# Weights in larger pieces on one queue, and the last attention job of segment 0 with its output projection one step sooner

## The chip, the cores and the metric

The kernel runs on one core of a Trainium2 chip. The metric is the time of the device in microseconds, from the start to the end of one execution; a profiled execution also gives the span from the first to the last instruction, and a record of every instruction. The engines are TensorE (PE; its weight loads are listed apart as PEld), VectorE (DVE), ScalarE (ACT), GpSimd (POOL) and SyncE (SP), which here only issues DMAs and DMA transposes.

## The reference

One block of a transformer for 2048 tokens of width 448 in bf16. A conditioning vector gives scales and shifts for two layer norms and gates for two residuals. The attention has 16 heads of width 28 and works in 4 segments of 512 tokens: inside a segment it is causal, and across segments it reads a memory that is summed up from the keys and values of the segments before.

```python
mod = (_silu(c) @ w_mod).reshape(c.shape[0], 6, 1, -1)      # sa, ca, ga, sb, cb, gb
h = _layernorm(x) * (1 + ca) + sa
x = x + ga * _A_ref(h, A_wq, A_wk, A_wv, A_wo, A_beta)
h = _layernorm(x) * (1 + cb) + sb
x = x + gb * _B_ref(h, B_w_gate, B_w_up, B_w_down)

# in _A_ref, for each segment s, with phi(t) = t + 1 if t > 0 else exp(t)
p = softmax(qs @ ks^T * scale + mask);  a_dot = p @ vs
a_mem = (phi(qs) @ M) / (phi(qs) @ z + 1e-6)
o = g * a_mem + (1 - g) * a_dot
M = M + phi(ks)^T @ vs;  z = z + phi(ks).sum
# in _B_ref
h = sigmoid(x @ w_gate) * (x @ w_up);  out = h @ w_down
```

## The kernel before

**Tiles.** Activations lie as 128 tokens by 448 columns (x_sb, four tiles to a segment) or transposed, as hT with the 448 columns in four chunks (k) of partitions by 512 tokens. Heads go in four groups of four; a pair (s, hc) names head group hc of segment s. PSUM has four rotating banks for everything but the logits, all from the pool ps_m: a matmul group that takes a bank waits until its last user was evacuated, four groups earlier. The logits have a buffer of their own (lg) of four banks, one buffer: a group of logits waits for the exponential of the group before.

**Head of the program.** The weights Wq, Wk, Wv and the first modulation columns are loaded, the first layer norm is taken, and the weights are multiplied by the scale of the layer norm (pad_copy, line 657, by DVE for Wq and Wk: chunks 0 to 3 of Wq, then Wk) while PE makes the bias rows (bias_rows, line 664) from the unscaled weights. Wq and Wk are first staged in the buffer that later holds the Down weights, so in the profile they are named wd_sb. The DMAs of a program share eight completion semaphores in turn: one that is issued waits on the eighth before it.

**Loop.** For each segment s, each head group hc and each group g of key blocks (block 0; blocks 1 and 3; block 2): logits, then ACT takes the exponential into pT, then GpSimd sets the masked corner of each block to zero (mask, line 437). For a head group that is done with its logits there follow, during the next one: mem_read (phi of the queries times the memory, tile mem, evacuated by DVE as r, t at lines 478 to 482), pv (probabilities times values, 40 matmuls into acc, evacuated as r, t at lines 457 to 463), the sum of both into ou (464), and otr (the transpose of ou into oT, issued on SP, 498).

**Order.** The program is not scheduled by a tool: the Python order is the order on each engine. Between logits and the rest a queue of jobs, fill, is run: the projections of later segments, the memory update dM, Wo, Gate, Up and Down. run_fill takes jobs until their costs have used up the pace of the step. Work on DVE and GpSimd that nothing on PE needs at once is put off with later(ns, fn, tag), and done when a counted clock (tick) has passed its due time, or when need(tag) asks for it. The masks are due 2600 ns after their logits, phi 4300 after its exponential.

**Around the change.** The queue at segment 1 starts with the last V projection of segment 2, the q and k projections of segment 3 for group 0, the memory update and prep_b2 (the columns of LN2). At step (1, 0, 2) the planner rebuilds the queue: two of the jobs that are left, then the four Wo tiles of segment 0 (wo_jobs), then memory keys, the rest, and Gate and Up. wo_tile multiplies oT by Wo for 128 tokens into pwo, and wo_fin adds the residual (520), takes the statistics (269, 270), the inverse root on GpSimd (rs, 273 and 274), and puts off the normalization xn (277, 281), each followed by a transpose into hT on SP (287). After the last tile four modulations of hT on DVE (291) are put off by 6500 ns and more. The first Gate matmul (gps, 542) reads hT, and Up (ups, 547 and 559) follows.

```python
                if prev[0] >= 0 and (g == 1 or ...) and prev in todo:
                    todo.remove(prev)
                    pv(*prev)
```

Of the kernel before, what the change touches and what calls it, by code (L numbers as in the profile page):

```python
# [13 lines left out]
P = 128  # L14
# [3 lines left out]
def kernel(  # L18
# [16 lines left out]
    nc = tc.nc  # L35
    _, S, D = A_x.shape
# [7 lines left out]
    DP, LW = NK * P, D - 3 * P  # L44
# [22 lines left out]
    def m_f32(name):  # L67
        return ps_m.tile([P, 512], F32, tag="m", name=name)
# [7 lines left out]
    def later(ns, fn, tag):  # L76
        deferred.append((clock[0] + ns, len(deferred), fn, tag))

    def run_deferred(pick):
        while True:  # L80
            due = [d for d in deferred if pick(d)]
            if not due:
                return
            d = min(due, key=lambda d: d[:2])
            deferred.remove(d)
            d[2]()

    def tick(ns):
        clock[0] += ns
        run_deferred(lambda d: d[0] <= clock[0])  # L90

    def need(*tags):
        for tag in tags:
            late_ = [d for d in deferred if d[3] == tag]
            if late_:
                print("forced", tag, len(late_), max(d[0] for d in late_) - clock[0])
            run_deferred(lambda d: d[3] == tag)
# [39 lines left out]
    wq_st = wd_sb[:, 0:NK, :]  # L137
    wk_st = wd_sb[:, NK:2 * NK, :]

    def load_w(eng, dst, w):  # L140
        eng.dma_start(dst[:, 0:3, :], w[0:3 * P, :].rearrange("(k p) n -> p k n", p=P))
        eng.dma_start(dst[0:LW, 3, :], w[3 * P:D, :])
# [6 lines left out]
    for b in wm_bufs:  # L149
        nc.vector.memset(b[:, NK * D:], 0.0)  # L150
    for st, w in ((wq_st, A_wq), (wk_st, A_wk)):
        other = nc.scalar if w is A_wq else nc.sync
        nc.sync.dma_start(st[:, 0:2, :], w[0:2 * P, :].rearrange("(k p) n -> p k n", p=P))
        other.dma_start(st[:, 2, :], w[2 * P:3 * P, :])
        other.dma_start(st[0:LW, 3, :], w[3 * P:D, :])
    load_w(nc.sync, wv_sb, A_wv)

    def load_wo():
# [25 lines left out]
    for hs in range(4):  # L184
        nc.gpsimd.affine_select(out=bmask[:, :, hs, :], in_=bmask[:, :, hs, :], compare_op=ALU.is_ge,
                                fill=0.0, base=-HP * hs, pattern=[[0, NHC], [0, ME]], channel_multiplier=1)
        nc.gpsimd.affine_select(out=bmask[:, :, hs, :], in_=bmask[:, :, hs, :], compare_op=ALU.is_ge,
                                fill=0.0, base=HP * hs + Dh - 1, pattern=[[0, NHC], [0, ME]],
# [251 lines left out]
    def pv(s, hc):  # L440
        u = (s, hc)
        need(("mask", u))
        pT = pT_of.pop(u)
        vt = vt_all[s]
        acc = m_f32("acc")
        accv = acc[:].rearrange("p (t h e) -> p t h e", h=4, e=HP)
        for qb in range(TPS):
            for hs in range(4):
                for kb in range(qb + 1):
                    c0 = OFF[kb] + (qb - kb) * P  # L450
                    nc.tensor.matmul(accv[:, qb, hs, 0:ME], lhsT=pT[:, hs, c0:c0 + P],  # L451
                                     rhs=vt[:, kb, hc * 4 + hs, 0:ME], start=(kb == 0), stop=(kb == qb))
        ou = ou_bufs[(s * NHC + hc) % 2]
        ou_of[u] = ou
        ouv = ou[:].rearrange("p t h e -> p (t h) e")[:, :, 0:Dh]
        r1 = work.tile([P, TPS, 4], F32, tag="r1", bufs=2)
        nc.vector.tensor_tensor(r1[:], accv[:, :, :, Dh], cb(0, hc), ALU.mult)
        nc.vector.reciprocal(r1[:], r1[:])
        if s == 0:
            nc.vector.tensor_tensor(ouv, num(acc), bc(r1), ALU.mult)  # L460
            return
        t1 = work.tile([P, TPS * 4, Dh], BF16, tag="t1", bufs=1)
        nc.vector.tensor_tensor(t1[:], num(acc), bc(r1), ALU.mult)
        later(1400, lambda: nc.vector.tensor_tensor(ouv, t1[:], t2_of.pop(u)[:], ALU.add), ("ou", u))
# [19 lines left out]
    def cb(i, hc):  # L484
        return coef[:, i:i + 1, hc * 4:(hc + 1) * 4].to_broadcast([P, TPS, 4])

    def bc(r):
        return r[:].rearrange("p t (h o) -> p (t h) o", o=1).to_broadcast([P, TPS * 4, Dh])

    def num(a):  # L490
        return a[:].rearrange("p (th e) -> p th e", e=HP)[:, :, 0:Dh]
# [116 lines left out]
    fill = deque()  # L608
# [107 lines left out]
    for k in range(NK):  # L716
        r = P if k < 3 else LW
        w = wv_sb[0:r, k, :]
# [47 lines left out]
    def cost(jobs):  # L766
        return sum(cst for cst, _ in jobs)
# [4 lines left out]
    todo = {(s, hc) for s in range(NSEG) for hc in range(NHC)}  # L772
    for s in range(NSEG):
        for hc in range(NHC):
            prev = (s, hc - 1) if hc else (s - 1, NHC - 1)
            for g in range(3):
                logits(s, hc, g)
                tick(450)
                if fill and fill[0][1] is gate_up2:
                    fill.popleft()[1]()  # L780
                    tick(6 * MM)
                    debt -= 6 * MM
                if prev[0] > 0 and g == 0:
                    mem_read(*prev)
                    tick(250)
                if prev[0] >= 0 and (g == 1 or g == 0 and s > 0 and (hc > 1 or s > 1) and pace[0] + debt <= 0) and prev in todo:
                    todo.remove(prev)
                    pv(*prev)
                    tick(1000)
                if prev[0] >= 0 and g == 2 and hc == 0:  # L790
                    otr(*prev)
                if (s, hc, g) in ((1, 0, 2), (2, 1, 0), (3, 1, 0)):
                    gj = gu_jobs(s - 1)
                    tail = list(fill)
                    print("left", s, cost(tail), len(tail))
                    fill.clear()
                    while tail and tail[0][1] is gate_up2:
                        fill.append(tail.pop(0))
                    if s == 1:
                        fill.extend(tail[:2])  # L800
                        tail = tail[2:]
                    for w in wo_jobs(s - 1):
                        fill.append(w)
                        if tail and s > 1:
                            fill.extend(tail[:2])
                            tail = tail[2:]
                    fill.extend((m[s][0:1] if s < 3 else []) + tail)
                    if s >= 2:
                        dj = down_jobs(s - 2)
                        if s == 2:  # L810
                            gj = gj[:8] + m[2][1:] + gj[8:]
                        fill.extend(dj + h2_jobs(s - 1) + gj)
                    else:
                        fill.extend(h2_jobs(s - 1) + gj[:8] + m[1][1:] + gj[8:])
                    pace[0] = (cost(fill) - KEEP[s] * GU) / (13, 12, 9)[s - 1]
                debt = run_fill(pace[0] + debt)
                if debt > 0:
                    print("dry", s, hc, g, debt)
                    debt = 0.0
                if g == 2 and hc > 0:  # L820
                    otr(*prev)
# [53 lines left out]
```

## Time and profile before

| | before |
|---|---|
| median of 3 runs | 254.08 us (253.94 to 255.12) |
| profiled execution | 253.74 us |
| its span | 252.0 us, 5339 instructions |
| mean granted TensorE clock | 0.992 |
| PE busy | 243.2 us (96%) |
| DVE, ACT, POOL busy | 173.8, 139.0, 74.1 us |
| DMA | 19.66 MB, mean 78 GB/s |

How to read the rows in what follows. A row of a timeline has the start and the length in microseconds from the start of the span, the engine, the line of the code, the operation with output and input, the shape, and how many instructions in succession it stands for (x4); in brackets stands how long the engine was idle before it and what released it. A q behind an engine's name (SPq, ACTq) marks an instruction of its queue, such as the issue of a DMA. A row of the list of waits has the total time, the number of times and the longest. A row of the table by windows has the length of the window, the busy time of PE, PEld, DVE, ACT and POOL, the granted clock as a share of the full one, the share of the DMA engines' time, and GB/s. In the row PEclk each digit is a fortieth of the span, 6.3 us, in tenths.

### The profile page before, as it was taken

The numbers are of one execution on the slowest core, as the hardware profiler recorded it, in microseconds if no ns is written. First come the engines' busy times: TensorE is split into PE (matmuls) and PEld (weight loads), VectorE is DVE, ScalarE is ACT, GpSimd is POOL, SyncE is SP. The second block draws the span as 40 slices with busy tenths as digits, with TensorE's granted clock in tenths as the row PEclk, the third lists the DMA queues.
The fourth block names the chain that finished last, engine by engine and source line by source line (L and its number), as shares of the span: only waits on it lengthen the run. The fifth ranks groups of instructions, "written<-read, shape, count | busy, mean of one in ns | idle before, by whom it ended". The sixth has DMA issues, their size and how long they took to land.

```text
span 252.0 us, 5339 instructions
## 1 busy us (share of the span) xinstructions
PE 243.2 (96%) x2083; PEld 115.1 (46%) x2083; DVE 173.8 (69%) x419; ACT 139.0 (55%) x173; POOL 74.1 (29%) x140
## 2 busy tenths in 40 slices
PE   7899999999988999999999999999999999999995
PEld 2434545446533445445434355454344455333354
DVE  6878899884887786489867666896565486544412
ACT  2158879978895977666375848552653300133300
POOL 4359144232553222344513141471120023000000
PEclk9999999999997999999999999999999999999999
DMA  5999996593035311102432210113210005100011
GB/s 147 288 269 279 348 253 111 90 203 54 3 62 68 62 34 10 23 0 48 95 79 44 42 23 0 25 38 84 57 22 3 3 20 120 36 0 0 3 36 36
DMA packets 41168, 19.66 MB, mean 78 GB/s; under 512 B 30008, under 2 KB 40248, under 8 KB 41144
## 3 DMA queue, kind: packets, MB, share of 16 engines
q1 hardware_dynamic: 38408, 17.61, 30.8%
q10 hardware_dynamic: 2736, 1.72, 2.4%
q8 instruction: 16, 0.26, 0.4%
q14 instruction: 8, 0.07, 0.1%
HBM read 10.67 MB, written 1.84 MB: 50 GB/s over the span
## 4 chain that ended last, share of the span: by engine, by line
PE 52%; DVE 7%; POOL 1%; DMA 1%; ACT 1%; issue 1%; DVEq 0%; POOLq 0%
PE ups L559 13%; PE dps L574 13%; PE gps L542 12%; PE gps L547 5%; PE acc L451 3%; PE pwo L510 2%; PE lg L424 2%; DVE fT L562 1%; DVE st L269 1%; DMA hT<-xn 1%; DVE x_sb L520 1%; DVE t L482 1%; PE dM L397 1%; PE ups L547 1%; PE mem L475 1%
## 5 line engine op out<-in xcount | busy, mean ns | idle before, releaser
L427 ACT ACTIVATE pT<-lg 128x2048 bf16<-128x2048 f32 (+1 forms) x48 | 76.8, 1601 | 25.8 <-PE lg L424 25.5
L562 DVE SCALAR_TENSOR_TENSOR fT<-tt,ups 128x512 bf16<-128x512 f32 x56 | 37.3, 687 | 39.5 <-PE ups L559 37.5
L437 POOL TENSOR_SCALAR_AFFINE_SELECT pT<-pT 128x512 bf16<-128x512 bf16 x64 | 40.7, 653 | 69.2 <-ACT pT L427 69.2
L550 ACT ACTIVATE tt<-gps 128x512 f32<-128x512 f32 x56 | 30.4, 594 | 54.8 <-PE gps L547 54.8
L574 PE MATMUL dps<-wd_sb,fT 128*128 128x448 bf16 (+1 forms) x238 | 43.7, 341 | 0.0
L542 PE MATMUL gps<-hT,wg_sb 128*128 128x512 bf16 x168 | 41.6, 384 | 0.0
L559 PE MATMUL ups<-hT,wu_sb 128*128 128x512 bf16 x168 | 41.1, 381 | 0.0
L574 PEld LDWEIGHTS <-fT 128*128 128x128 bf16 x238 | 22.9, 98 | 18.7
L542 PEld LDWEIGHTS <-wg_sb 128*128 128x128 bf16 x168 | 15.8, 99 | 18.1 <-issue 1.0
L559 PEld LDWEIGHTS <-wu_sb 128*128 128x128 bf16 x168 | 14.1, 97 | 21.7 <-issue 7.9
L451 PE MATMUL acc<-vt,pT 128*128 128x29 bf16 x640 | 18.6, 176 | 2.1 <-POOL pT L437 1.7
L269 DVE BATCH_NORM_STATS2 st<-x_sb 128x6 f32<-128x448 bf16 x32 | 19.7, 617 | 0.5
L451 PEld LDWEIGHTS <-pT 128*128 128x128 bf16 x640 | 17.7, 96 | 5.2 <-POOL pT L437 2.4
L547 PE MATMUL ups<-hT,wgu_sb 64*128 64x512 bf16 x56 | 17.8, 382 | 0.8 <-ACT tt L550 0.5
L273 POOL TENSOR_SCALAR rs<-mv 128x1 f32<-128x1 f32 (+2 forms) x21 | 5.3, 252 | 44.8 <-DVE mv L270 43.7
L424 PE MATMUL lg<-qT,kT 28*128 28x512 bf16 (+3 forms) x256 | 17.3, 302 | 0.4 <-ACT pT L427 0.4
L343 PE MATMUL pq<-hT,wq_sb 128*128 128x512 bf16 x64 | 17.0, 380 | 0.0
L547 PE MATMUL gps<-hT,wgu_sb 64*128 64x512 bf16 x56 | 16.9, 381 | 0.0
L343 PE MATMUL pq<-hT,wk_sb 128*128 128x512 bf16 x64 | 16.4, 379 | 0.0
L277 DVE TENSOR_SCALAR xn<-x_sb,mv,rs 128x448 bf16<-128x448 bf16 x32 | 14.4, 471 | 2.6 <-POOL rs L274 2.6
L576 DVE TENSOR_TENSOR ot<-dps,x_sb 128x448 bf16<-128x448 f32 (+1 forms) x17 | 9.9, 590 | 9.0 <-PE dps L574 9.0
L274 POOL TENSOR_TENSOR rs<-rs,mhalf 128x1 f32<-128x1 f32 (+2 forms) x21 | 14.2, 675 | 1.7
(101 smaller groups left out, 258.1 us busy)
## 6 DMA issues: line engine op xcount, KB each, us to landing
wm<-in_w_mod_dram SPq DMA_DIRECT2D x4, 392.0 KB, 5.3
x_sb<-in_A_x_dram SPq DMA_DIRECT2D x3, 448.0 KB, 5.3
wd_sb<-in_B_w_down_dram SPq DMA_DIRECT2D x3, 448.0 KB, 9.7
wg_sb<-in_B_w_gate_dram SPq DMA_DIRECT2D x3, 448.0 KB, 9.4
wu_sb<-in_B_w_up_dram SPq DMA_DIRECT2D x3, 448.0 KB, 10.2
out_dram<-ot SPq DMA_DIRECT2D x8, 112.0 KB, 1.8
out_dram<-ot ACTq DMA_DIRECT2D x7, 112.0 KB, 1.7
wm<-in_w_mod_dram SPq DMA_DIRECT2D x2, 196.0 KB
```

The source lines that it names most:

```text
L269: nc.vector.bn_stats(st[:], self.srcs[i])
L343: nc.tensor.matmul(pq[:, 0:L], lhsT=head_cols(w_sb, k, hc), rhs=h[:, k, :], start=(k == 0), stop=(k == NK - 1))
L424: nc.tensor.matmul(lg[:, hs, wid:wid + nq], lhsT=kT[r, hc, kb * P:(kb + 1) * P], rhs=qT[r, hc, kb * P:L], start=True, stop=True, tile_posi ...
L427: nc.scalar.activation(pT[:, :, w0:w0 + wid], lg[:, :, 0:wid], AF.Exp, scale=scale)
L437: nc.gpsimd.affine_select(out=blk, in_=blk, compare_op=ALU.is_ge, fill=0.0, base=0, pattern=[[0, 4], [1, P]], channel_multiplier=-1)
L451: nc.tensor.matmul(accv[:, qb, hs, 0:ME], lhsT=pT[:, hs, c0:c0 + P], rhs=vt[:, kb, hc * 4 + hs, 0:ME], start=(kb == 0), stop=(kb == qb))
L542: nc.tensor.matmul(g[:, 0:L], lhsT=wg_sb[:, k, f], rhs=h[:, k, :], start=(k == 0), stop=False)
L547: nc.tensor.matmul(dst[:, 0:L], lhsT=wgu_sb[r:r + LW, f], rhs=h[r:r + LW, 3, :], start=first, stop=not first, tile_position=(r, 0))
L550: nc.scalar.activation(tt[:], g[:, 0:L], AF.Tanh, scale=0.5)
L559: nc.tensor.matmul(u[:, 0:L], lhsT=wu_sb[:, k, f], rhs=h[:, k, :], start=False, stop=(k == 2))
L562: nc.vector.scalar_tensor_tensor(ft[:], tt[:], 1.0, u[:, 0:L], op0=ALU.add, op1=ALU.mult)
L574: nc.tensor.matmul(dp[:, c], lhsT=fT_of[(s, fc)][:, t * P:(t + 1) * P], rhs=wd_sb[:, fc, c], start=(fc == 0), stop=(fc == NFC - 1))
```

## The change

Three edits.

First, the loads of Wq and Wk into their staging buffers. Before: chunks 0 and 1 together, chunk 2 and the 64 rows of chunk 3, for Wk all on SP, for Wq the two small ones on the ACT queue. Now: chunks 0 to 2 of each in one DMA, then the 64 rows of each, all on SP. There are two DMAs fewer, so each later load waits on a DMA that was issued earlier.

Second, pv of (0, 3) goes from step (1, 0, 1) into the queue of step (1, 0, 0), behind its first job, and otr of (0, 3) from g = 2 to g = 1 of segment 1.

Third, at (1, 0, 2) one job stands ahead of the first Wo tile where two did. The job passed over, a K projection, follows the Wo tiles.

```diff
     for st, w in ((wq_st, A_wq), (wk_st, A_wk)):
-        other = nc.scalar if w is A_wq else nc.sync
-        nc.sync.dma_start(st[:, 0:2, :], w[0:2 * P, :].rearrange("(k p) n -> p k n", p=P))
-        other.dma_start(st[:, 2, :], w[2 * P:3 * P, :])
-        other.dma_start(st[0:LW, 3, :], w[3 * P:D, :])
+        nc.sync.dma_start(st[:, 0:3, :], w[0:3 * P, :].rearrange("(k p) n -> p k n", p=P))
+    for st, w in ((wq_st, A_wq), (wk_st, A_wk)):
+        nc.sync.dma_start(st[0:LW, 3, :], w[3 * P:D, :])
...
-                if prev[0] >= 0 and g == 2 and hc == 0:
+                if (s, hc, g) == (1, 0, 0):
+                    todo.remove(prev)
+                    def early(prev=prev):
+                        pv(*prev)
+                        tick(1000)
+                    fill.insert(1, (0, early))
+                if prev[0] >= 0 and g == (1 if s == 1 else 2) and hc == 0:
                     otr(*prev)
...
                     if s == 1:
-                        fill.extend(tail[:2])
-                        tail = tail[2:]
+                        fill.append(tail.pop(0))
```

The first loads on SP before, with the semaphore on which each waits; wd_sb is the staging buffer, and x_sb the tokens of segment 1:

```order
L153 DMA wd_sb<-in_A_wq_dram 128x2x448
L153 DMA wd_sb<-in_A_wk_dram 128x2x448 [waits DMAHW0_49]
L154 DMA wd_sb<-in_A_wk_dram 128x448 [waits DMAHW1_49]
L155 DMA wd_sb<-in_A_wk_dram 64x448 [waits DMAHW2_49]
L141 DMA wv_sb<-in_A_wv_dram 128x3x448 [waits DMAHW4_49]
L142 DMA wv_sb<-in_A_wv_dram 64x448 [waits DMAHW6_49]
L104 DMA x_sb<-in_A_x_dram 128x4x448 [waits DMAHW7_49]
```

And of the change:

```order
L152 DMA wd_sb<-in_A_wq_dram 128x3x448
L152 DMA wd_sb<-in_A_wk_dram 128x3x448 [waits DMAHW0_49]
L154 DMA wd_sb<-in_A_wq_dram 64x448 [waits DMAHW1_49]
L154 DMA wd_sb<-in_A_wk_dram 64x448 [waits DMAHW2_49]
L141 DMA wv_sb<-in_A_wv_dram 128x3x448 [waits DMAHW3_49]
L142 DMA wv_sb<-in_A_wv_dram 64x448 [waits DMAHW4_49]
L104 DMA x_sb<-in_A_x_dram 128x4x448 [waits DMAHW5_49]
```

The last 64 rows of Wq, which were on the ACT queue, now stand third on SP, on the semaphore that the third load waited on before; Wv and x_sb each wait on a semaphore that stands earlier in the turn.

GpSimd before, from the masks of (1, 0) to those of (1, 2); pT_924, pT_1097 and pT_1275 are the probabilities of (1, 0), (1, 1) and (1, 2), rs and mv belong to LN2 of segment 0:

```order
L437 AFFINE_SELECT pT_924<-pT_924 128x4x128 x3
L273 TENSOR_SCALAR rs_1124<-mv_1123 128x1
L274 TENSOR_TENSOR rs_1124<-rs_1124,mhalf_121 128x1
...
L437 AFFINE_SELECT pT_1097<-pT_1097 128x4x128
L273 TENSOR_SCALAR rs_1124<-mv_1123 128x1
L274 TENSOR_TENSOR rs_1124<-rs_1124,mhalf_121 128x1
L437 AFFINE_SELECT pT_1097<-pT_1097 128x4x128 x3
L437 AFFINE_SELECT pT_1275<-pT_1275 128x4x128 x4
```

And of the change, where the same probabilities are pT_922, pT_1102 and pT_1275:

```order
L436 AFFINE_SELECT pT_922<-pT_922 128x4x128 x2
L272 TENSOR_SCALAR rs_1096<-mv_1095 128x1
L273 TENSOR_TENSOR rs_1096<-rs_1096,mhalf_119 128x1
L436 AFFINE_SELECT pT_922<-pT_922 128x4x128
...
L272 TENSOR_SCALAR rs_1096<-mv_1095 128x1
L273 TENSOR_TENSOR rs_1096<-rs_1096,mhalf_119 128x1
L436 AFFINE_SELECT pT_1102<-pT_1102 128x4x128 x4
L436 AFFINE_SELECT pT_1275<-pT_1275 128x4x128 x4
```

The fourth rs pair stood ahead of three masks of (1, 1); now all four pairs stand ahead of all four of them, and eight masks follow in succession.

DVE before, from the last statistics of LN2 of segment 0 to its modulations; mem_1284 is the memory read of (1, 1), e_1249 the phi of a key group:

```order
L270 BN_AGGR mv_1123<-st_1225 128x2
L277 TENSOR_SCALAR xn0_127<-x_sb_76,mv_1123,rs_1124 128x448
L281 COPY xn0_127<-xn0_127 128x64
L464 TENSOR_TENSOR ou0_129<-t1_1211,t2_1115 128x16x28
L277 TENSOR_SCALAR xn0_127<-x_sb_76,mv_1123,rs_1124 128x448
L281 COPY xn0_127<-xn0_127 128x64
L478 SCALAR_TENSOR_TENSOR r2_1289<-mem_1284,coef_155 128x16
L479 RECIPROCAL r2_1289<-r2_1289 128x16
L482 TENSOR_TENSOR t2_1292<-mem_1284,r2_1289 128x448
L369 TENSOR_SCALAR r_1300<-kT1_159 128x512
L370 TENSOR_TENSOR e_1249<-e_1249,r_1300 128x512
L291 TENSOR_SCALAR hT_1165<-hT_1165,cols_125 128x512 x4
```

And of the change, where they are mem_1285 and e_1250, and e_1109 is the phi that mem_1285 reads:

```order
L368 TENSOR_SCALAR r_1222<-qT1_81 128x512
L369 TENSOR_TENSOR e_1109<-e_1109,r_1222 128x512
L276 TENSOR_SCALAR xn0_125<-x_sb_76,mv_1095,rs_1096 128x448
L280 COPY xn0_125<-xn0_125 128x64
L463 TENSOR_TENSOR ou0_127<-t1_1217,t2_1119 128x16x28
L290 TENSOR_SCALAR hT_1146<-hT_1146,cols_123 128x512 x3
L477 SCALAR_TENSOR_TENSOR r2_1290<-mem_1285,coef_153 128x16
L478 RECIPROCAL r2_1290<-r2_1290 128x16
L481 TENSOR_TENSOR t2_1293<-mem_1285,r2_1290 128x448
L290 TENSOR_SCALAR hT_1146<-hT_1146,cols_123 128x512
L368 TENSOR_SCALAR r_1302<-kT1_157 128x512
L369 TENSOR_TENSOR e_1250<-e_1250,r_1302 128x512
```

The memory evacuation (r2, t2) and the phi of the keys stood ahead of the four modulations; now three modulations stand ahead of the evacuation and all four ahead of the phi.

## The prediction

> **What bounds the kernel now.** I read the page first: busy times, the granted clock by slices, the chain of waits.
>
> ```profile
> PE 243.2 (96%) x2083; PEld 115.1 (46%) x2083; DVE 173.8 (69%) x419; ACT 139.0 (55%) x173; POOL 74.1 (29%) x140
> PEclk9999999999997999999999999999999999999999
> PE 52%; DVE 7%; POOL 1%; DMA 1%; ACT 1%; issue 1%; DVEq 0%; POOLq 0%
> ```
>
> PE is busy for 243.2 of 252.0 us, so little is to be won, in two places: where PE stands still, and where it is busy at less than full clock. One slice, the thirteenth (75.6 to 81.9 us), shows 7. The list of PE's waits names the stops:
>
> ```profile
> PE acc L451 <- POOL pT L437: 1.7, 1, 1.7
> PE warm L664 <- DMA wd_sb<-in_A_wq_dram: 0.4, 1, 0.4
> ```
>
> The change has a hand in exactly these two. The timeline of PE around the first:
>
> ```profile
> 61.76 1.03 PE L343 MATMUL pq<-hT,wk_sb 128*128 128x512 bf16 x4
> ...
> 71.95 0.39 PE L475 MATMUL mem<-rm,e 128*128 128x116 bf16 x4
> 72.17 2.44 PE L355 MATMUL pv<-wv_sb,hT 128*128 128x448 bf16 x12
> 74.54 0.40 PE L424 MATMUL lg<-qT,kT 28*128 28x384 bf16 x8
> 76.61 1.20 PE L451 MATMUL acc<-vt,pT 128*128 128x29 bf16 x40 [1.68 <-POOL pT L437]
> 77.66 1.65 PE L355 MATMUL pv<-wv_sb,hT 128*128 128x448 bf16 x4
> 79.17 2.13 PE L542 MATMUL gps<-hT,wg_sb 128*128 128x512 bf16 x6
> ...
> 81.24 0.39 PE L547 MATMUL ups<-hT,wgu_sb 64*128 64x512 bf16 x1
> ...
> 83.71 0.40 PE L424 MATMUL lg<-qT,kT 28*128 28x512 bf16 x4 [0.25 <-ACT pT L427]
> ...
> 84.26 1.46 PE L542 MATMUL gps<-hT,wg_sb 128*128 128x512 bf16 x6
> ```
>
> PE stops for 1.68 us at acc of (1,1). Behind that stop the first Gate pair (gps at 79.17) takes 2.13 us, where the second (84.26) takes 1.46. The table by one-us windows says why; its last column but two is the granted clock:
>
> ```profile
> 77.00:78.00 1.00, 1.00 (x33) 0.78 (x30) 0.25 (x1) 1.00 (x2) 0.26 (x1) 0.57 0.34 68
> ...
> 80.00:81.00 1.00, 1.00 (x5) 0.40 (x3) 0.93 (x4) 0.00 (x0) 0.00 (x0) 0.73 1.05 11
> ```
>
> The two windows between them show 0.50. So some 3.4 us (77.1 to 80.5) ran at half clock, begun half a us after PE resumed: 0.43 + 0.50 + 0.50 + 0.27 = 1.7 us of PE work not done. From mem at 71.95 to ups at 81.24 are 9.29 us. The work in it at full clock, start to start: mem 0.22, pv 2.37 for three, lg 0.39, acc 1.05, one more pv 0.79, gps 1.46, together 6.28. The other 3.0 us are the stop (1.68) and the clock (1.33).
>
> But is PE the bound in that stretch? I followed the first Gate pair back on VectorE (DVE), SyncE's queue (SP) and GpSimd (POOL):
>
> ```profile
> 73.05 0.28 POOL L273 TENSOR_SCALAR rs<-mv 128x1 f32<-128x1 f32 x1 [2.66 <-DVE mv L270]
> ...
> 74.16 2.43 POOL L437 TENSOR_SCALAR_AFFINE_SELECT pT<-pT 128x512 bf16<-128x512 bf16 x4
> ```
> ```profile
> 74.23 0.69 DVE L277 TENSOR_SCALAR xn<-x_sb,mv,rs 128x448 bf16<-128x448 bf16 x1 [0.46 <-POOL rs L274]
> ...
> 75.36 0.16 DVE L478 SCALAR_TENSOR_TENSOR r<-mem,coef 128x16 f32<-128x16 f32 x1
> ...
> 78.45 1.63 DVE L291 TENSOR_SCALAR hT<-hT,cols 128x512 bf16<-128x512 bf16 x4 [1.20 <-DMA hT<-xn]
> 80.00 0.16 DVE L457 TENSOR_TENSOR r<-acc,coef 128x16 f32<-128x16 f32 x1
> ```
> ```profile
> 75.47 1.20 SPq L287 DMA_TRANSPOSE hT<-xn  x1
> ```
>
> There is a second chain, as long as PE's: the fourth token tile's normalization (xn, 74.23), its transpose (issued 75.47, ready 2.98 later at 78.45), four modulations (1.55), then the evacuation of acc (r, t from 80.00) that frees the bank which ups takes at 81.24. From xn to ups this is 81.24 - 74.23 = 7.01 us. So much of the stop and of the slow clock was covered by a chain that would have held PE anyway: to take the stop away is not to gain 3 us. What decides is when the fourth xn comes, and what stands behind it.
>
> **The head.** Before, the last 64 rows of Wq were issued by ScalarE (ACT), late; what waits:
>
> ```profile
> 8.02 0.53 ACTq L155 DMA_DIRECT2D wd_sb<-in_A_wq_dram  x1
> ```
> ```profile
> 10.55 0.58 DVE L657 TENSOR_SCALAR wq_sb<-wd_sb,cols 128x448 bf16<-128x448 bf16 x2
> ...
> 12.55 0.33 DVE L657 TENSOR_SCALAR wq_sb<-wd_sb,cols 64x448 bf16<-64x448 bf16 x1 [0.40 <-DMA wd_sb<-in_A_wq_dram]
> ```
> ```profile
> 5.05 0.47 SPq L154 DMA_DIRECT2D wd_sb<-in_A_wk_dram  x1
> ```
>
> In the new order the piece stands third on SP, behind the same semaphore as the load at 5.05, so it is issued some 3 us sooner than 8.02. It took at most 12.55 - 8.02 = 4.5 us; by that it is there at 9.6, with 2.5 us to spare before DVE comes to it at 12.15. The 0.40 us go: everything behind is in order on DVE and PE. The first piece of Wq grows by half (336 KB for 224) and is wanted at 10.55, 8.2 us after its issue; the page's list of DMA issues has 6.7 for 224 KB, so it should just fit. Bounds: -0.40 and 0 (if the larger pieces only trade one late piece for another). I take **-0.40**.
> The Trainium skill speaks against this edit ("DMA: Bandwidth & Descriptors", Issuing engines are not separate DMA queues): transfers started by different engines share the same 16 DMA engines, and spreading them saves only the time on the sequencer. By it alone, moving from ACT to SP would give 0 and the sum would come out 0.40 higher; but here it was the late issue on ACT, at 8.02, that the row shows, and that is the part which the rule leaves open.
>
> **pv and transpose of (0,3) earlier.** No work is added: 40 matmuls of acc move ahead of two projections and a logits group, one transpose is issued earlier on SP. DVE was idle ahead of its part, so that is hidden. The transpose was issued here:
>
> ```profile
> 59.97 1.19 SPq L498 DMA_TRANSPOSE oT<-ou  x1
> ```
>
> Two projections and eight matmuls of logits, some 2.1 us, now stand behind acc instead of ahead of it, so the issue comes at 57.8, and with the 2.98 that a transpose took at 75.47 it is ready at 60.8. The first Wo tile, its reader, now stands at 62: 1.2 us of cover, and any lateness beyond that would be a stop of PE one for one. ACT is the cost:
>
> ```profile
> 58.56 1.92 ACT L427 ACTIVATE pT<-lg 128x2048 bf16<-128x2048 f32 x1
> 61.01 1.02 ACT L427 ACTIVATE pT<-lg 128x1024 bf16<-128x1024 f32 x1 [0.53 <-PE lg L424]
> ```
>
> The exponential of (1,0,1), at 58.56, ran without a gap behind two casts of projections that now come one acc (1.05) later; ACT was behind PE there, which takes up a part of that. The next logits group needs the exponential's end, 60.48 before, and stood ahead of 61.01 less the 0.53 that ACT then waited for it. Price +0.2 for PE, an estimate between 0 (ACT takes up all) and +0.5 (half of the 1.05 comes through).
>
> **The first Wo tile sooner.** It takes the place of a projection at 61.76, with the 0.2 just found 61.96. What matters is DVE's row of work from there to the fourth xn:
>
> ```profile
> 63.47 0.17 DVE L478 SCALAR_TENSOR_TENSOR r<-mem,coef 128x16 f32<-128x16 f32 x1 [1.59 <-PE mem L475]
> ...
> 64.51 0.61 DVE L520 TENSOR_TENSOR x_sb<-pwo,x_sb 128x448 bf16<-128x448 f32 x1
> ...
> 65.92 0.59 DVE L520 TENSOR_TENSOR x_sb<-pwo,x_sb 128x448 bf16<-128x448 f32 x1
> ...
> 67.30 0.59 DVE L520 TENSOR_TENSOR x_sb<-pwo,x_sb 128x448 bf16<-128x448 f32 x1
> ...
> 68.69 0.38 DVE L277 TENSOR_SCALAR xn<-x_sb,mv,rs 128x448 bf16<-128x448 bf16 x1
> ...
> 69.20 0.17 DVE L457 TENSOR_TENSOR r<-acc,coef 128x16 f32<-128x16 f32 x1
> ...
> 70.23 0.39 DVE L277 TENSOR_SCALAR xn<-x_sb,mv,rs 128x448 bf16<-128x448 bf16 x1
> ...
> 70.74 0.29 DVE L369 TENSOR_SCALAR r<-qT 128x512 bf16<-128x512 bf16 x1
> ...
> 71.46 0.62 DVE L520 TENSOR_TENSOR x_sb<-pwo,x_sb 128x448 bf16<-128x448 f32 x1
> ```
>
> Start to start: a tile's residual and statistics 1.38, a memory evacuation (r, t from mem) 1.04, an xn with its copy 0.51, an acc evacuation 1.03, the two operations on qT (phi) 0.72. In the new order four of the first, one memory evacuation, three xn, one acc evacuation and one phi stand ahead of the fourth xn: 5.52 + 1.04 + 1.53 + 1.03 + 0.72 = 9.84, begun at the end of the first Wo tile (61.96 + 0.9, so 62.9). The fourth xn starts at **72.7**, 1.5 us sooner than before. GpSimd can delay that: the last rs pair now ends near 71, and four masks follow at once, 2.43 us. An xn under the masks lasted 0.69 where one without lasted 0.38, and it and its copy 1.13 for 0.51. I allow up to 0.9 for the operations that meet them: 72.7 to 73.6.
>
> From that xn to ups it was 7.01. The new order puts into this chain what stood beside it: three modulations now stand ahead of the memory evacuation of (1,1), and modulations wait for the transposes. So 1.04 and the phi behind it, 0.72, come on top: 8.77, or 8.15 if no mask falls on the xn. ups starts at 80.9 to 82.4, for 81.24 before: -0.3 to +1.2, and I take **+0.45**. The gain at the fourth xn is eaten by two pieces of DVE work that the transposes used to cover.
>
> **Where the stop goes.** acc of (1,1) no longer waits: its masks don't stand behind a late rs. But mem of (1,1) now waits for the phi, which ends where the fourth xn starts, at 72.7 to 73.6, while PE is there at 72.15: a stop of 0.55 to 1.45. Then the first Gate pair takes the bank which the late memory evacuation frees, and ups waits again, since a modulation, a phi and an acc evacuation (0.39 + 0.72 + 1.03) follow while PE has only 1.46 to do: 0.7. All stops together are the time to ups less the work: 80.9 to 82.4, less 72.15, less 6.28, or 2.5 to 4.0 us; that leaves 1.2 to 1.85 at the Gate pair, as long as the 1.68 after which the clock fell. A new half-clock stretch would then lie later, from about 80 to 83.4, behind the chain, and not under it. It loses 1.7 less the 0.7 of the stop at ups; with the case that it doesn't come, bounds 0 and 1.7, I take **+0.9**.
> The Trainium skill says that the clock is halved after at least one idle window of about 3.4 us ("TensorE: Matmul & The Clock Gate", Part 1: The HAM clock gate). The row differs: 1.68 us of standing were followed by 3.4 us at half clock, and the measurement decides. By the page's rule no stop forecast here would do it, and the sum would be 0.9 lower.
>
> Behind 84 us only places in time change; PE has no stop to take up a delay there, so it reaches the end whole. **Sum:** -0.40 + 0.45 + 0.9 = +0.95 (the 0.2 is within the second term). The profiled execution took 253.74, so 254.7; the median of the runs is 254.08, 0.34 above it, so **255.0**. A measurement of this kernel can tell about 0.5% from no change: under 252.8 is faster, over 255.35 slower.
>
> **The rivals.**
> Full clock throughout: three stops of which each stays under 1.68 leave the clock alone, the chain comes at its early end, and the logits group at 83.71 without its 0.25: -0.40 - 0.3 - 0.25 = -0.95, 253.1 (252.4 to 254.1). For it: the stops of 0.4 us did nothing to the clock. Against: the Gate stop at its longest passes 1.68, and two stops lie close together.
> Slower: GpSimd's masks. Eight now run almost in a row from 71, each bf16 operation of DVE that meets one lasts 0.3 longer, the chain comes at its late end (+1.2) and the half-clock stretch falls behind ups whole (+1.7): -0.4 + 1.2 + 1.7 = +2.5, 256.6. It decides if the first Gate matmul starts after 80.2. For it: the 0.69 for 0.38. Against: before, the phi at 70.74 ran without a mask.
> It does nothing: the larger pieces land as late as the old ones, and the chain gives no more and no less than before: 254.1.
>
> **Chances.** Forecast 0.48 (its own range 254.0 to 256.0; three in five of it within 0.5%, the rest slower: 0.29 and 0.19), full clock 0.28 (0.12 of it below 252.8), slower by masks 0.20, nothing 0.04. A gain at the head beyond 0.4 moves 0.02 from same to faster. Faster 0.12 + 0.02 = 0.14; same 0.29 + 0.16 + 0.04 - 0.02 = 0.47; slower 0.19 + 0.20 = 0.39. The range, with half of the masks' case and most of the full clock's in it: 252.6 to 256.8.
>
> **What would show it.** Right: no wait for wq in PE's list; the fourth xn of LN2 of segment 0 at 72 to 73.5 (all times less 0.4 from the head); no wait at acc (1,1), one at mem (1,1) and one at gps; half clock in windows behind 79. Wrong: gps before 78.5 at full clock, or a stop at the first Wo tile because the transpose of (0,3) came too late, which would break all that follows.

## The result: no difference that can be measured

| | before | changed |
|---|---|---|
| first comparison | 254.26 us (253.94 to 255.12, 4 runs) | 254.31 us (254.11 to 254.51, 4 runs) |
| ratio | | 0.9997 (0.997 to 1.0024) |
| second comparison | 253.99 us (253.25 to 254.98, 29 runs) | 254.22 us (253.75 to 255.99, 12 runs) |
| ratio | | 1.0015 (0.9995 to 1.0034) |
| profiled execution, span | 253.74, 252.0 us | 254.51, 252.8 us |

The forecast was 255.0 with a range of 252.6 to 256.8. The time lies in the range and is 0.7 us below the forecast, and behind the "no difference" stand large terms of both signs. From the page of the changed kernel, busy time and granted clock:

```profile
span 252.8 us, 5338 instructions
PE 242.3 (96%) x2083; PEld 114.8 (45%) x2083; DVE 173.9 (69%) x419; ACT 139.5 (55%) x173; POOL 73.8 (29%) x140
PEclk9999999999999999999999999999999999999999
```

The slice with 7 is gone: the clock stayed full. PE is busy 0.9 us less than before, since no stretch runs slowly, and the span is 0.8 us longer, so PE stands 1.7 us more. Where, the list of its waits tells:

```profile
PE gps L541 <- DVE t L481: 1.4, 1, 1.4
PE mem L474 <- DVE e L369: 1.1, 1, 1.1
PE ups L546 <- DVE t L462: 0.7, 2, 0.4
PE dM L396 <- DMA pk<-e: 0.5, 1, 0.5
```

The two waits of before (acc 1.7, wq 0.4) are away; the stop at mem and the one at the Gate pair stand in their place, as forecast, and a wait at dM that was not. The timeline of PE in the stretch:

```profile
61.92 0.92 PE L509 MATMUL pwo<-wo_sb,oT 128*128 128x448 bf16 x4
...
73.49 0.39 PE L474 MATMUL mem<-rm,e 128*128 128x116 bf16 x4 [1.14 <-DVE e L369]
...
76.41 1.17 PE L450 MATMUL acc<-vt,pT 128*128 128x29 bf16 x40
...
79.79 1.46 PE L541 MATMUL gps<-hT,wg_sb 128*128 128x512 bf16 x6 [1.44 <-DVE t L481]
...
81.88 0.39 PE L546 MATMUL ups<-hT,wgu_sb 64*128 64x512 bf16 x1 [0.31 <-DVE t L462]
...
84.03 0.40 PE L423 MATMUL lg<-qT,kT 28*128 28x512 bf16 x4
```

And DVE, from the fourth xn to the evacuation that frees the bank of ups; the memory evacuation (t, L481) waits behind three modulations, and these 3.08 us for the transposes:

```profile
73.35 0.70 DVE L276 TENSOR_SCALAR xn<-x_sb,mv,rs 128x448 bf16<-128x448 bf16 x1
...
77.65 1.06 DVE L290 TENSOR_SCALAR hT<-hT,cols 128x512 bf16<-128x512 bf16 x3 [3.08 <-DMA hT<-xn]
...
79.11 0.62 DVE L481 TENSOR_TENSOR t<-mem,r 128x448 bf16<-128x448 f32 x1
...
81.19 0.62 DVE L462 TENSOR_TENSOR t<-acc,r 128x448 bf16<-128x448 f32 x1
```

There are 48 groups of logits on PE, which makes them a ruler. Their starts in the timeline, less the starts of the same groups before (each kernel's profiled execution; minus is sooner):

| logits group, at before | changed | e1 head | e2 planner | e3 modulations | e4 filler | e8 held masks | e10 phi |
|---|---|---|---|---|---|---|---|
| 54.37 | -0.48 | -0.49 | -0.10 | -0.47 | 0.10 | -0.48 | -0.47 |
| 62.72 | 0.05 | -0.49 | 0.55 | 0.33 | 0.10 | 0.26 | -0.44 |
| 74.54 | 1.54 | -0.49 | 2.04 | 1.82 | 1.61 | 1.19 | 0.49 |
| 83.71 | 0.32 | -0.07 | 0.54 | -1.38 | 0.22 | -2.01 | -2.70 |
| 127.21 | 0.33 | -0.06 | 0.55 | -1.37 | 0.23 | -2.00 | -2.69 |
| 135.35 | 0.85 | 0.67 | 0.55 | -0.84 | 0.23 | -1.47 | -3.00 |
| 183.93 | 0.92 | 0.73 | 0.56 | -0.78 | 0.24 | -1.42 | -2.94 |

The changed kernel is 0.48 us ahead up to 55 us, loses all of it and more by 84, stays as it is for 45 us, and loses another 0.5 at 130 to 136.

The fall of the clock is not a property of a kernel but of an execution. Each execution lists its mean granted clock: 0.991 to 0.993 where it had the half-clock stretch, 0.998 to 1.000 where not. Before had it in 25 of 29 executions beside e1 to e4, in 16 of 29 beside e5 to e8 and in 4 of 7 beside e9 and e10.

So the medians mix two things. At equal clock the two kernels are not level: in the second comparison the 9 executions of the changed kernel that kept the clock have a median of 254.12 us, the 13 of before 253.45. The change costs 0.67 us there, and that it loses the clock less often hides it.

### The profile page after: what moved, and what is told of

Its sections match the earlier page's. It is cut to its first block, busy times and chain, and to the rows that moved or that the text cites. A ratio compares the mean times of both kernels' runs of the same rounds, so it can differ in the third digit from the quotient of the medians.

```text
span 252.8 us, 5338 instructions
## 1 busy us (share of the span) xinstructions
PE 242.3 (96%) x2083; PEld 114.8 (45%) x2083; DVE 173.9 (69%) x419; ACT 139.5 (55%) x173; POOL 73.8 (29%) x140
## 3 DMA queue, kind: packets, MB, share of 16 engines
q10 hardware_dynamic: 2512, 1.55, 2.1%
## 4 chain that ended last, share of the span: by engine, by line
PE 50%; DVE 8%; POOL 1%; DMA 1%; ACT 1%; issue 1%; DVEq 0%; POOLq 0%
PE ups L558 13%; PE dps L573 13%; PE gps L541 11%; PE gps L546 5%; PE acc L450 2%; PE pwo L509 2%; PE lg L423 2%; DVE fT L561 2%; DVE st L268 1%; DMA hT<-xn 1%; DVE x_sb L519 1%; DVE t L481 1%; PE dM L396 1%; PE ups L546 1%; PE mem L474 1%
## 5 line engine op out<-in xcount | busy, mean ns | idle before, releaser
L541 PE MATMUL gps<-hT,wg_sb 128*128 128x512 bf16 x168 | 40.9, 379 | 1.4 <-DVE t L481 1.4
```

Source lines behind the costliest of these rows:

```text
L541: nc.tensor.matmul(g[:, 0:L], lhsT=wg_sb[:, k, f], rhs=h[:, k, :], start=(k == 0), stop=False)
```

## The experiments

Each kernel was run in several executions beside the kernel before on the same chip: e1 to e4 on one chip, e5 to e8 on a second, e9 and e10 on a third. At full clock before took 253.75, 253.45 and 253.47 us there (4, 13 and 3 executions), so differences across sets are good to some 0.3 us.

**e1, the loads alone.**

```diff
-        other = nc.scalar if w is A_wq else nc.sync
-        nc.sync.dma_start(st[:, 0:2, :], w[0:2 * P, :].rearrange("(k p) n -> p k n", p=P))
-        other.dma_start(st[:, 2, :], w[2 * P:3 * P, :])
-        other.dma_start(st[0:LW, 3, :], w[3 * P:D, :])
+        nc.sync.dma_start(st[:, 0:3, :], w[0:3 * P, :].rearrange("(k p) n -> p k n", p=P))
+    for st, w in ((wq_st, A_wq), (wk_st, A_wk)):
+        nc.sync.dma_start(st[0:LW, 3, :], w[3 * P:D, :])
```

> The kernel before with the first edit alone (the loads of Wq and Wk). Theory: the late issue on the ACT queue was the whole cause of the 0.40 us wait, and everything behind is in order, so all logits groups come 0.48 us sooner up to the end, with the stop at acc of (1,1) and the half-clock stretch unchanged: 0.4 to 0.5 us less than before, ratio 0.998. Rival: the stretch at 72 to 84 us takes the gain up, because GpSimd or DVE there follow something other than PE: ratio 1.000.

Measured: 253.17 us, ratio 0.9963 (0.9946 to 0.998). The gain of 0.49 is there, to the group at 74.54. In the profiled execution the rival is then right: the stop at acc is as long as ever, and half clock costs more than it did in the profile of before (2.92 for 2.13 at the Gate pair). Another 0.7 is lost between 127 and 136 us (the table):

```profile
76.13 1.15 PE L450 MATMUL acc<-vt,pT 128*128 128x29 bf16 x40 [1.68 <-POOL pT L436]
...
78.09 2.92 PE L541 MATMUL gps<-hT,wg_sb 128*128 128x512 bf16 x6
```

Over 12 executions neither statement holds. Only 5 lost the clock (median 253.86, the others 253.05), while 25 of 29 of before did (254.52, the others 253.75). So at equal clock the loads alone are worth 0.7 us in this set, 0.2 more than the wait that they remove, and fewer executions lost the clock. Only four executions of before at full clock stand behind the 0.7; against the 13 of the next set it would be 0.4. Where the rest comes from, and why the clock fell less often behind a stop of the same length, stays open. Nor does e1 separate the two parts of the edit, the larger pieces and the move of the 64 rows to SP.

**e2, the planner's part alone**: the second and third edits, with the loads of before.

> The kernel before with the second and third edits alone (early pv and transpose, first Wo tile sooner). Theory: the planner's part costs what the profile of the change shows less the head, 0.32 + 0.48 = 0.8 us by the logits group at 84 us, and up to 0.5 more behind 130 us: 0.8 to 1.3 us over before, ratio 1.003 to 1.005. Rival: the planner's part is neutral, and the profiled pair was far apart by chance: ratio 1.000.

Measured: 254.80 us, ratio 1.0033 (1.0011 to 1.0055). The theory holds: early pv and earlier Wo make the kernel slower. At full clock it is 254.51 for 253.75, 0.76 us; five of 12 executions lost the clock, and those stand at 255.91.

**e3, the order on DVE undone.**

```diff
-                later(6500 + 400 * kc, lambda kc=kc: ln.modulate(kc, 2), ("ln2", s))
+                later((8500 if s == 0 else 6500) + 400 * kc, lambda kc=kc: ln.modulate(kc, 2), ("ln2", s))
```

> The changed kernel with the four modulations of LN2 of segment 0 due 2000 ns later, so that the memory evacuation of (1,1) and the phi of the keys stand ahead of them on DVE again. Theory: the 1.44 us stop at the first Gate pair and the 0.31 at ups are made by that order. DVE is idle for 3.08 us ahead of the modulations and takes both in there; the Gate pair then starts about 78.1 and ups about 80.3 instead of 81.88, so 1.6 us less than the change: about 252.7 us, ratio to before 0.993 to 0.995. Rival: the transposes of hT set the Gate pair, and the order hides behind them: less than 0.5 us gained, ratio 0.998 or more.

Measured: 252.42 us, ratio 0.9933 (0.9907 to 0.9959). The theory holds. DVE of this kernel, and then PE:

```profile
75.26 0.62 DVE L481 TENSOR_TENSOR t<-mem,r 128x448 bf16<-128x448 f32 x1
...
77.05 1.38 DVE L290 TENSOR_SCALAR hT<-hT,cols 128x512 bf16<-128x512 bf16 x4 [0.45 <-DMA hT<-xn]
```
```profile
78.47 1.46 PE L541 MATMUL gps<-hT,wg_sb 128*128 128x512 bf16 x6
79.86 0.39 PE L546 MATMUL gps<-hT,wgu_sb 64*128 64x512 bf16 x1
79.86 0.39 PE L546 MATMUL ups<-hT,wgu_sb 64*128 64x512 bf16 x1
```

The memory evacuation and the phi stand in the time in which DVE waited for the transposes. No bracket is left at the Gate pair or at ups: both stops were made by the order of nine DVE instructions.

**e4, work in the place of the stop**, in the kernel before:

```diff
-        for k in range(NK):
+        for k in [k for _ in range(3 if (s, t) == (3, 2) else 1) for k in range(NK)]:
             nc.tensor.matmul(pv[:, 0:D], lhsT=h[:, k, t * P:(t + 1) * P], rhs=wv_sb[:, k, :],
```

> The kernel before, with the third V projection of segment 3 computed three times into the same bank (8 matmuls more, 1.6 us of PE work) ahead of the stop at acc of (1,1), so that PE works where it stood. Theory: no stop, so no half-clock stretch, but ups still waits for the chain from the fourth xn over the transposes, modulations and the evacuation of acc: within 0.2 us of before although the clock stays at 1.00. Rival: the half clock cost PE its 1.33 us, and with the clock kept the time falls by about 1.3 us, ratio 0.995.

Measured: 253.76 us, ratio 0.9976 (0.9963 to 0.9989), and all 12 executions at full clock. PE of this kernel:

```profile
76.72 1.16 PE L451 MATMUL acc<-vt,pT 128*128 128x29 bf16 x40 [0.17 <-POOL pT L437]
...
79.47 0.39 PE L542 MATMUL gps<-hT,wg_sb 128*128 128x512 bf16 x1 [0.82 <-DVE hT L291]
```

The stop at acc is filled with 8 matmuls that nobody needs, and PE now waits for the modulations instead: the second chain is real. But the kernel is 0.6 us faster than before by the ratio, more than the 0.2 of the theory and less than the 1.3 of the rival. It takes just what before takes in the executions that keep their clock (253.75), and 0.76 less than those that lose it (254.52). So the chain covers a little under half of the 1.33 us of slow clock that the profile of before shows, not nearly all.

**e5, the changed kernel again.**

> The changed kernel itself in more executions, for the share of them in which TensorE's clock falls (a mean granted clock of 0.991 to 0.993 where 0.998 to 1.000 means that it did not), and as the measure for the others. Theory: its stops, at most 1.44 us each, keep the clock in nearly all executions; before, the 1.68 us stop lost it in 25 of 29, and that cost 0.77 us there (254.52 for 253.76). The median is 254.1 to 254.5, ratio 0.998 to 1.000. Rival: the four executions seen so far were lucky, the clock falls in a third or more, and those stand 1 us or more above the rest.

Measured: 254.22 us, ratio 1.0015 (0.9995 to 1.0034). Of 12 executions 9 kept the clock (median 254.12) and 3 lost it (255.43, 1.3 us more), so 3 of 16 with the four of the first comparison. This lies between the two: the clock was not kept in nearly all executions, but lost in fewer than a third, and those that lost it stand as far above the rest as the rival said. The median is where the theory had it, the ratio a little above. The profiled one is one of the three. PE, and two windows (the last number but two is the clock):

```profile
79.48 2.72 PE L541 MATMUL gps<-hT,wg_sb 128*128 128x512 bf16 x6 [1.47 <-DVE t L481]
```
```profile
80.00:81.00 1.00, 1.00 (x4) 0.30 (x3) 0.88 (x4) 0.00 (x0) 0.00 (x0) 0.50 0.00 0
81.00:82.00 1.00, 1.00 (x3) 0.15 (x1) 0.90 (x3) 0.00 (x0) 0.00 (x0) 0.50 0.29 60
```

This is the stretch that the prediction described, at its place: the Gate stop is 1.47 us here and was 1.44 in the execution that kept its clock.

**e6, the change without the third edit**: two jobs ahead of the first Wo tile.

```diff
-                        fill.append(tail.pop(0))
+                        fill.extend(tail[:2])
+                        tail = tail[2:]
```

> The change without its third edit: loads, and early pv and transpose, but two jobs ahead of the first Wo tile as before. Theory: the early pv costs the 0.46 us wait at dM and 0.2 us at the logits behind it, and gives nothing, since acc of (1,1) keeps its stop of 1.7 us: 0.3 to 0.6 us over the loads alone (253.17), ratio 0.998 to 0.999. Rival: the early pv is what takes the stop away, and the wait at acc is gone from the list.

Measured: 254.15 us, ratio 1.0002 (0.9984 to 1.002). The stop at acc is there as before:

```profile
76.43 1.16 PE L450 MATMUL acc<-vt,pT 128*128 128x29 bf16 x40 [1.68 <-POOL pT L436]
```

So the third edit took it away, not the early pv, and the early pv gives nothing: at full clock 253.80, where the loads alone took 253.05 beside another set of runs. That is 0.75 over the loads, more than the 0.3 to 0.6 expected. Its profile shows 0.3 us lost by the logits of (1,0,2), ahead of which dM takes 1.29 us for 1.00 without a bracket; the rest of the difference was not traced.

**e7, the change without the second edit**: pv and transpose of (0,3) where they were.

```diff
-                if (s, hc, g) == (1, 0, 0):
-                    todo.remove(prev)
...
-                    fill.insert(1, (0, early))
-                if prev[0] >= 0 and g == (1 if s == 1 else 2) and hc == 0:
+                if prev[0] >= 0 and g == 2 and hc == 0:
```

> The change without its second edit: loads, and the first Wo tile one job sooner, but pv and transpose of (0,3) where they were. Theory: the two edits need each other; the transpose is issued at 59.5 and ready 2.98 later at 62.5, the first Wo tile stands at 61.3, so a stop of about 1.2 us at pwo, and the chain on DVE begins later by as much: ratio 1.002 to 1.005. Rival: the transpose is ready sooner than that (under 2.2 us), the stop is short, and without the early pv's 0.5 to 0.6 us the kernel is faster than the change: ratio 0.997 or less.

Measured: 254.20 us, ratio 1.0007 (0.9992 to 1.0022), all 12 executions at full clock. The theory's stop did not come, and the kernel is not faster than the change either, as the rival had it. SP, and then PE:

```profile
55.90 4.79 SPq L497 DMA_TRANSPOSE oT<-ou  x2
```
```profile
61.29 1.07 PE L509 MATMUL pwo<-wo_sb,oT 128*128 128x448 bf16 x4
...
81.13 0.39 PE L546 MATMUL ups<-hT,wgu_sb 64*128 64x512 bf16 x1 [0.92 <-DVE t L462]
```

The second transpose ended its issue at 60.69, and the first Wo tile runs at 61.29 without a wait that the profile shows: it was issued at 59.49, so it was ready after 1.8 us at most, not after the 2.98 that I had taken from another transpose. The edits do not need each other. But a faster first half only makes PE wait longer at ups (0.92): DVE's order still decides.

**e8, the masks held back**, on top of e3:

```diff
-                eng = nc.gpsimd if self.key[1] else nc.vector
+                eng = nc.gpsimd if self.key[1] or i == 3 else nc.vector
...
-            later(2600, lambda kb=kb: mask(pT, kb), ("mask", u))
+            later(4800 if u == (1, 1) else 2600, lambda kb=kb: mask(pT, kb), ("mask", u))
```

> The kernel of the experiment with later modulations, and beside it the four masks of (1,1) held back behind the fourth xn: that tile's copy of 64 columns is done by GpSimd, and the masks are due 2200 ns later, behind it. Theory: the masks ran from 71.1 to 73.9 and made DVE's copy, phi and xn longer (0.49 for 0.18, 0.68 for 0.43, 0.70 for 0.38, 0.9 us together); held back, the phi ends 0.5 sooner, mem of (1,1) waits 0.6 instead of 1.1, and the Gate pair and ups come 0.4 to 0.6 us sooner: 251.9 us, ratio 0.991. Rival: acc then waits for its masks, or the longer operations were not due to the masks: no gain over 252.4.

Measured: 251.75 us, ratio 0.9909 (0.989 to 0.9928). DVE, GpSimd and PE of this kernel:

```profile
72.19 0.18 DVE L280 COPY xn<-xn 128x64 bf16<-128x64 bf16 x1
...
72.66 0.43 DVE L369 TENSOR_TENSOR e<-e,r 128x512 bf16<-128x512 bf16 x1
73.00 0.39 DVE L276 TENSOR_SCALAR xn<-x_sb,mv,rs 128x448 bf16<-128x448 bf16 x1
```
```profile
73.74 3.21 POOL L436 TENSOR_SCALAR_AFFINE_SELECT pT<-pT 128x512 bf16<-128x512 bf16 x5
```
```profile
73.14 0.39 PE L474 MATMUL mem<-rm,e 128*128 128x116 bf16 x4 [0.58 <-DVE e L369]
...
77.83 1.46 PE L541 MATMUL gps<-hT,wg_sb 128*128 128x512 bf16 x6
```

The three operations have the lengths that they have without a mask, mem waits 0.58 for 1.14, the Gate pair comes 0.64 us sooner than in e3, and acc does not wait for the later masks. The theory holds.

**e9, e8 without the early pv** (the second edit undone as in e7), and **e10, e9 with one phi later** (the edit shown):

```diff
-            pq_of[u] = phi(qT[:, hc, :], 4300, ("pq", u))
+            pq_of[u] = phi(qT[:, hc, :], 5500 if u == (2, 3) else 4300, ("pq", u))
```

> The kernel of the experiment with held masks, without the second edit of the change: pv and transpose of (0,3) stand where they stood before. Theory: the early pv only costs (0.2 to 0.3 us at the logits of (1,0,2), in some executions 0.5 to 0.7 more at dM), and the first Wo tile did not wait for the later transpose in the experiment that left the early pv out: 0.2 to 0.9 us faster, 250.9 to 251.6 us, ratio 0.988 to 0.990. Rival: with the faster chain the early pv pays, and the time is the same or longer.

Measured: 251.48 us (251.44 to 251.53, 4 runs), ratio 0.9906 (0.9889 to 0.9922). Against e8 by way of before that is no measurable difference; the intervals cover each other. In the profiles e9 is 0.7 us ahead of e8 at 84 us, as the theory had it, since e8's had a dM wait of 0.7. Over all profiles dM waited in four of the six with the early pv (0.46 to 0.73 us) and was stretched to 1.3 us for 1.0 in the other two (e5, e6); in the six without it, it took 1.00 without a wait.

> The same, and the phi of the queries of (2,3) due 1200 ns later, so that on DVE it stands behind the evacuation of acc instead of ahead of it, at 133 to 136 us. Theory: in the profiles with the new loads this phi began just behind a mask and lasted until the mask's end (0.69 and 0.73 for 0.29 and 0.43), which made ups wait 0.4 us for the evacuation; the evacuation reads PSUM and is not slowed, so that wait goes: 0.4 us faster than the kernel beside it. Rival: the evacuation is slowed by the masks as well, or ups waits for something else: no difference.

Measured: 250.94 us (250.92 to 250.99, 4 runs), ratio 0.9885 (0.9866 to 0.9905), 0.54 us under e9, which ran beside it; the two sets do not overlap. e9, DVE and PE:

```profile
130.32 0.71 DVE L368 TENSOR_SCALAR r<-qT 128x512 bf16<-128x512 bf16 x1
```
```profile
132.88 0.39 PE L546 MATMUL ups<-hT,wgu_sb 64*128 64x512 bf16 x1 [0.44 <-DVE t L462]
```

And e10, where the evacuation stands first and ups has no bracket:

```profile
131.11 0.62 DVE L462 TENSOR_TENSOR t<-acc,r 128x448 bf16<-128x448 f32 x1
131.65 0.28 DVE L368 TENSOR_SCALAR r<-qT 128x512 bf16<-128x512 bf16 x1
```
```profile
132.04 0.38 PE L546 MATMUL ups<-hT,wgu_sb 64*128 64x512 bf16 x1
```

e10 beats both kernels: the loads, the earlier first Wo tile, and three due times and one copy beside them.

## Why the prediction came out as it did

**The number: near, in part by luck.** For the profiled execution the sum gave 254.7, and it took 254.51. But the terms were -0.48 at the head (-0.40 forecast), +1.12 for the chain (+0.45), nothing for the clock (+0.9), and 0.5 behind 84 us that the sum did not have; 0.3 were won at the logits of 84 us, which no longer wait. The single errors are about as large as the forecast change, and they cancel.

**The head: right, where it was looked at.** -0.40 forecast, -0.48 measured up to 55 us. The piece of Wq is issued where it was said and nobody waits; SP, then DVE of the changed kernel:

```profile
5.14 0.56 SPq L154 DMA_DIRECT2D wd_sb<-in_A_wq_dram  x1
```
```profile
12.07 0.32 DVE L656 TENSOR_SCALAR wq_sb<-wd_sb,cols 64x448 bf16<-64x448 bf16 x1
```

**Where the stop goes: right.** acc does not wait. mem stops 1.14 (0.55 to 1.45 forecast), the Gate pair 1.44 (1.2 to 1.85), ups 0.31 (0.7). e3 shows that the last two come from the modulations standing ahead of the memory evacuation, as the sum had it.

**The chain: right in kind, at its late end.** +0.45 was taken from -0.3 to +1.2. ups came at 81.88 for 81.24, and with the head's 0.48 that is +1.12. Two things made it late. The masks lengthened DVE's operations as the slower rival said (e8 takes that away: 0.64 us). GpSimd and DVE of the changed kernel; without a mask the copy takes 0.18 and the phi's second operation 0.43:

```profile
71.08 2.84 POOL L436 TENSOR_SCALAR_AFFINE_SELECT pT<-pT 128x512 bf16<-128x512 bf16 x4
```
```profile
71.97 0.50 DVE L280 COPY xn<-xn 128x64 bf16<-128x64 bf16 x1
...
72.75 0.68 DVE L369 TENSOR_TENSOR e<-e,r 128x512 bf16<-128x512 bf16 x1
```

And the stretch began later: the first Wo tile stands at 61.92, or 62.40 without the head's gain, where 61.96 was forecast, since dM waited 0.46 us for a transpose of the keys:

```profile
59.40 0.38 PE L396 MATMUL dM<-vt,pk 128*128 128x116 bf16 x4 [0.46 <-DMA pk<-e]
```

The early pv was priced for its own transpose's reader alone. That dM is late in all six profiles with the early pv and in none without it points to SP's other transposes, which come later beside an early one; the sum left that out.

**The clock: the step that failed.** The prediction took +0.9 because a Gate stop of 1.2 to 1.85 us is as long as the 1.68 after which the clock had fallen once. One profile cannot tell that the fall comes in some executions and not in others. The runs give shares (the stops as the one profile of each kernel has them): with a stop of 1.68 us 25 of 29, 16 of 29 and 4 of 7 (before), 5 of 12 (e1), 7 of 12 (e6); with 1.44 to 1.47, 3 of 16 (the change); with none over 0.82 in the stretch, none of 26 (e4, e8, e9, e10). Between these the length alone does not settle it: with 1.13 or 1.14 it was none of 12 (e7) and 1 of 6 (e3), and e2, with 1.1 at mem, 0.7 at the Gate pair and 0.8 at ups in its profile, had 5 of 12. So the change does not add a fall of the clock; it makes falls rarer. Before loses 0.8 to 0.9 us (in the two large sets) in more than half of its executions, the changed kernel 1.3 us in one of five. The last section shows what else decides beside the length: where the stop lies on the clock's steps. At equal clock the change is 0.67 us slower, nearly what the planner's part costs alone (e2, 0.76): the loads' 0.7 of e1 is not there beside it, and the rarer falls make up for a good part of the loss. Part of where the loads' gain goes stands below, under "Behind 84 us".
The rule that the prediction cited beside this (the Trainium skill, "TensorE: Matmul & The Clock Gate", Part 1: The HAM clock gate: half clock after at least one idle window of about 3.4 us) gave 0.9 less than the forecast, nearly what was measured; but stops of 1.47 and 1.68 us did halve the clock here, so its length does not hold for this kernel.

**"Much of the slow clock was covered": half right.** e4 keeps the clock and is 0.6 us faster than before, or 0.76 against the executions of before that lost it, so some 0.8 of the 1.33 us was bare.

**"Behind 84 us only places in time change": wrong by 0.5 us.** Two rows of DVE with the masks beside them, of before and then of the changed kernel:

```profile
132.89 0.29 DVE L369 TENSOR_SCALAR r<-qT 128x512 bf16<-128x512 bf16 x1
```
```profile
132.92 1.52 POOL L437 TENSOR_SCALAR_AFFINE_SELECT pT<-pT 128x512 bf16<-128x512 bf16 x2 [2.62 <-ACT pT L427]
```
```profile
133.34 0.69 DVE L368 TENSOR_SCALAR r<-qT 128x512 bf16<-128x512 bf16 x1
```
```profile
133.25 1.27 POOL L436 TENSOR_SCALAR_AFFINE_SELECT pT<-pT 128x512 bf16<-128x512 bf16 x2 [2.62 <-ACT pT L426]
```

Before, the phi began 0.03 us ahead of the mask and lasted 0.29; now it begins 0.09 behind it and lasts 0.69. Then ups waits 0.43. The order is the same, and a tenth of a microsecond decides. It comes with the loads: in all eight profiles that have the new loads and the old due time the phi begins 0.07 to 0.12 us behind the mask and ups waits 0.40 to 0.45, while in the three with the old loads it begins 0.03 ahead and ups does not wait. At 122 to 127 us DVE waits 0.62 or 0.63 for the transposes of hT in those three and 0.74 to 0.99 in all with the new loads, which is the tenth; why these transposes come later is open. So most of what the head wins is lost again here. e10 moves the phi out of the way and has the 0.4 back, and more.

**The rivals.** Full clock throughout came true for the clock in 13 of 16 executions, but not at the chain's early end. The masks were at work as the slower rival said, at the first Gate matmul 79.79 plus 0.48, just past its point of 80.2, but without its bare half-clock stretch in 13 of 16 executions. "It does nothing" has the nearest number, 254.1, for reasons that are wrong: the last piece of Wq came sooner, and the chain ended later.

## What to carry to other kernels

A wait of the busiest engine is worth the shorter of itself and the lead that it has over the next chain: follow the consumer behind the stop back through the other engines before a gain is booked, and where a job moves, look at what now stands ahead of each evacuation on the in-order engine that frees the banks. Work that another engine needs soon (an evacuation) belongs ahead of work that must wait for a DMA; here that order alone was worth 1.6 to 2.1 us (e3's ratio against the two of the change). And before a difference of half a per cent is explained from one profile a side, look at how often a rare event (a fall of the clock) comes in the runs, and compare the executions with it and those without it apart: here a cost of 0.67 us hid behind two nearly equal medians.

## What the runs showed of the hardware that I had not expected

Whether the clock falls after a stop of PE differs from one execution to the next: the same 1.68 us stop was followed by half clock in 25 of 29 executions of one set and in 16 of 29 of another. In each of the four profiles in which it fell it fell for 3.41 us.

The traces' records of the granted clock show more. In all twelve profiles every change of the clock lies a whole number of steps of 3.413 us from every other (before: 71.68, 3.41 and 170.67 us apart, so 21, 1 and 50 steps), and the steps lie at another place in each execution: the first change to full clock comes 4.36 to 6.81 us into the span. With PE's standing time counted for each step from there to the end of the span, all eight steps with 1.55 us or more were followed by half clock, none with 1.26 or less was, and of the two with 1.44 one was (e5) and one was not (the first profile of the changed kernel). So in these profiles it is the part of a stop that falls into one step that counts. A stop of 1.68 us at a random place puts 1.44 or more into one step in 65% of cases, an estimate: (3.41 - 1.68 + 2 x 0.24) / 3.41. Before, e1 and e6, which have that stop, lost the clock in 57 of 89 executions. The falls of e2 and e3, whose longest stop is 1.14 in their one profile, are not explained by it.

Some of DVE's bf16 operations from SBUF that begin while a mask runs on GpSimd last longer. Over the twelve traces the second operation of phi did in all 68 cases (0.67 to 0.89 us for 0.43), the copy of 64 columns in all 9 (0.49 for 0.18), the first operation of phi and xn in about four of five (0.69 for 0.29, 0.70 for 0.38). The phi that began 0.03 us ahead of a mask had its normal length. Not all are touched: the sum into ou kept its 0.39 in all 24 cases, and evacuations from PSUM in f32 their 0.62 in all 105.
